# Linear attention and GELU layers on one core: state products of the fourth pair moved into its attention run, v of the first pair released by the first alpha

## The chip, the core and the metric

The kernel runs on one core of a Trainium2 chip. Five engines with queues of their own work side by side: TensorE (PE, with its weight loads PEld), VectorE (DVE), ScalarE (ACT), GpSimd (POOL) and SyncE (SP). The metric is the device time of one execution in microseconds (us); the time shown for a kernel is the median of its runs.

## What is computed

A gated linear attention recurrence over 768 tokens for 4 batches of 8 heads of 48 columns, then two dense layers (384 to 2048 to 384) with a tanh GELU between them, on all 3072 tokens:

```python
for t in range(S):
    state = alpha[:, :, t, :, None] * state + np.einsum('bhd,bhe->bhde', k[:, :, t], v[:, :, t])
    y[:, :, t] = np.einsum('bhd,bhde->bhe', q[:, :, t], state)
x = y.transpose(0, 2, 1, 3).reshape(B * S, H * D)
h = x @ w_in
g = 0.5 * h * (1.0 + np.tanh(c * (h + 0.044715 * h * h * h)))   # c = sqrt(2 / pi)
out = g @ w_out
```

## The kernel before, in words

Tokens are cut into six chunks of 128; a *pair* is two batches of one chunk, a *unit* one batch of it. There are twelve pairs, numbered from 0 (the first pair is pair 0, the fourth is pair 3); pair 2c + i holds batches 2i and 2i + 1 of chunk c.

One unit goes so. ACT takes the logarithm of alpha (`la`, L396 and L398); PE sums it over the tokens with a triangular matrix (`cum`, L383 and L387 for the packed pairs 0 and 1, L415 and L417 later); ACT makes b = exp(cum) and binv = exp(-cum) (L449) and, up to pair 2, the decay at the chunk's end (`bend`, L438). DVE makes q' = q b and k' = k binv (`qp`, `kp`, L477). Both are turned to have the columns on partitions: on PE with an identity and copied out of PSUM to `qkT` up to pair 4 (L487 and L518, copies L505 and L525), and from pair 5 on by a DMA transpose that SP issues (L545). In pairs 0 and 1 k' is also turned back to natural order (`kn`, L533, L540). The attention products k' q' (L582, `at`) are masked on DVE (L589, `atm`). The output y is the masked attention times v (L640, or L648 for a pair at once), and from chunk 1 on also q' times the carried state. The state is carried by a product of k' and v (L599, `kv`) and one or two DVE steps (L622, L625).

q' times the carried state is made in one of two ways. For pairs in the tuple `CARRIED` it stands inside the attention run: sixteen products of 64 rows by 48 columns (L562) into two PSUM banks that stay held until y is copied out as two parts of x (L658). For pair 3, not in the tuple, it is four products of 96 columns per unit (L637) in that unit's own y run (copy L664). x is turned (L671 and `xT` L675; by DMA L551 from pair 6 on) and feeds layer 1 (L683, `hT`), GELU on ACT (L689, `gT`), layer 2 (L702, `acc`), a copy (L714, `ot`) and the store (L727).

PSUM has three rings: `ff` (four banks: hT, acc, products of zeros, some sums and attention), `yk` (two banks: turns, state products, y) and `ca` (one pair of banks). `fill` (L317) multiplies zeros on PE into a spare bank; these results are not used.

The order of the work is decided when the program is built. A scheduler walks a hand-written list, `FIRST`, whose entries name an engine and a task (`P:cum0.0` is the sums of pair 0, unit 0, on PE; `P:fill.7` seven products of zeros), and places everything after it by the planner's costs (`W`, `COST`), due times (`prio`, changed by `SHIFT`) and extra dependences (`AFTER`). Each engine then runs its queue in that order, and waits only for semaphores. `LANDED` holds the times at which the planner takes the first 34 loads to have landed; it moves nothing on the chip but the plan.

Loads: a, q and k of the first two pairs are twelve strips, `load.0` to `load.11`, one batch each, issued by SP (one by ACT) at once in the order of `RINGS`; the last is k of pair 1, unit 1. All others stand in `LOADS`, on GpSimd's queue. A gate there is a one-column copy on GpSimd that waits for a tile, and so holds all that is queued behind it:

```python
def wait(self, r, m, j):
    u = self.p[list(self.p)[m]]
    return lambda e: self.nc.gpsimd.tensor_copy(self.gate[:, 0:1], u[r][:, j, 0, 0:1])
```

The first gate, `gatea 0 1`, waits for alpha of pair 0, unit 1, and lets v of pair 0 go (`load.12`, 384 KB). The second, `gatek 0 1`, waits for k of pair 0, unit 1, and lets the first quarter of `w_in` go, v of pair 1, the other weights and the later pairs.

Of the kernel before, what the change touches and what calls it, by code (L numbers as in the profile page):

```python
# [13 lines left out]

W = dict(**{'in': 2400},
    ln=745, exp=705, bend=170, gelu4=485, gelu2=340, table=1290,
    cum=530, cum_packed=1500, t8=450, t4=225, attn=340, kv=170, inter=165, intra=203, tx=168, l1_4=655, l1_2=340, l2=651,
    qk2=880, qk1=500, ev8=610, ev4=350, mask=610, st=1065, st0=545, end=110, attn2=600, vb=320, vb_act=480, ring=1300, ring_issue=670, out=2050, lead=600, receipt=1400, receipt_hw=1000, xc=475, xe=275, ot=540,
    ev8_act=920, ev4_act=520, xc_act=385, xe_act=400, ot_act=450,
    strip=1700, cast=1450, weight=2080, dma=2100, issue=1100, wissue=760, sp=420, store=2600, turn=1250, landed=2200, xbar_qk=1500, xbar_x=1400, turn_lead=50, stored=300, turn_receipt=200, rows=1826, ones=205, late_qk=1700, late_x=1700, late_x6=500, piece=330, late_k=1500, piece_issue=450, begin=620, cast_0=1300, share=1200, cast_1=1900, ln_packed=1040, cold=380, t64=640, fill=216, zero=1100,  # L20
)
COST = {
    ("ACT", "b"): (385, 135), ("ACT", "binv"): (385, 135), ("ACT", "ev"): (600, 40), ("ACT", "gelu"): (510, 110),
# [151 lines left out]
class _Kernel:  # L175
# [3 lines left out]

    SPLIT = (2,)  # L180
    EARLY = (0, 1)
    LOADS = ('gatea 0 1', 'v0', 'gatek 0 1', 'in 0', 'v1', 'in 1', 'in 2', 'in 3', 'out 0', 'out 1', '2a', 'out 2', '2b', 'out 3', '3', '4', '5', '6', 'a7', 'q7', 'hold k 5', 'k7', 'v7', 'a8', 'hold k 6', 'q8', 'k8', 'a9', 'hold k 7', 'v8', 'q9', 'k9', 'hold k 8', 'v9', 'a10', 'q10', 'hold x 7', 'k10', 'a11', 'hold k 9', 'q11', 'k11', 'v10', 'hold k 10', 'v11')

    PACKED, CUM_FF, R = (0, 1), (0, 1), 4
    RINGS = (('a', 0, 0, 1), ('a', 0, 1, 2), ('q', 0, 0, 1), ('k', 0, 0, 1), ('q', 0, 1, 2), ('k', 0, 1, 2),
# [1 line left out]
    BY_ACT = (2,)  # L187

    FIRST = """
        S:load.0 S:load.1 S:load.3 A:table.0 A:load.2 A:ln0.0 S:load.4 S:load.5 P:fill.7 G:gate.0 G:load.12 S:load.6 S:load.7 S:load.8 P:fill.2 P:cum0.0  # L190
        A:ln0.1 A:b0.0 P:cum0.1 V:qp0.0 P:t0.0 P:fill.1 A:binv0.0 A:bend0.0 V:kp0.0 S:load.9 A:b0.1 S:load.10 A:binv0.1 A:bend0.1 V:end0.0 V:qp0.1 V:kp0.1
        A:ev0.0 P:fill.3 P:t0.1 A:ev0.1 G:gate.1 P:t0.2 S:load.11 P:t0.3 A:ln1.0 V:ev0.2 G:load.13 G:load.14 A:ev0.3 P:attn0.0 A:ln1.1 V:mask0.0 V:mask0.1
        P:t0.4 P:t0.5 A:ev0.4 P:attn0.1 V:mask0.2 P:cum1.0 V:mask0.3 V:vb0.0 P:cum1.1 A:ev0.5 P:fill.1 P:fill.1 P:y0.0 G:load.15 P:kv0.0 G:load.16 A:binv1.0
        A:bend1.0 G:load.17 A:b1.0 V:vb0.1 A:x0.0 P:tx0.0 A:binv1.1 V:qp1.0 V:st0.0 A:bend1.1 A:b1.1 G:load.18 V:xe0.0 V:kp1.0 V:qp1.1 G:load.19 G:load.20
        P:fill.1 G:load.21 P:y0.1 P:t1.0 P:fill.1 V:end1.0 A:x0.1 P:t1.1 A:ev1.0 A:ev1.1 P:t1.2 G:load.22 V:kp1.1 P:tx0.1 V:xe0.1 P:attn1.0 A:ev1.2 G:load.23
        V:mask1.1 V:mask1.0 P:t1.3 P:kv0.1 A:ev1.3 V:st0.1 P:l10.0 P:t1.4 A:vb1.0 P:l10.1 A:vb1.1 V:ev1.4 P:y1.0 V:x1.0 P:attn1.1 P:t1.5 P:kv1.0 A:gelu0.0
        P:l10.3 V:mask1.3 V:mask1.2 A:ev1.5 P:l10.2 P:y1.1 A:gelu0.1 G:load.24 V:st1.0 A:gelu0.3 P:tx1.0 P:l10.5 A:gelu0.2 V:x1.1 A:gelu0.5 G:load.25 P:tx1.1
        V:xe1.0 V:xe1.1 P:l10.4 A:gelu0.4 P:l11.0 P:l11.3 G:load.26 G:load.27 A:gelu1.0 P:l10.6 P:l11.4 A:gelu1.3 G:load.28 P:l10.7 A:gelu0.6 A:gelu1.4
        A:gelu0.7 P:l11.1 P:l11.5 A:gelu1.1 P:l11.6 P:l11.2 A:gelu1.5 A:gelu1.6 A:gelu1.2 P:l11.7 A:gelu1.7 G:load.29 G:load.30 P:kv1.1 P:l20.2 A:ln2.0
        P:l20.6 P:l20.0 P:l20.3 P:cum2.0 A:binv2.0 A:b2.0 P:l20.1 G:load.31 P:l20.10 A:ln2.1 V:kp2.0 P:l20.4 V:qp2.0 P:t2.0 A:bend2.0 P:cum2.1 A:b2.1 P:l20.8  # L200
        P:l20.5 A:binv2.1 V:st1.1 P:l20.7 V:kp2.1 A:bend2.1 A:ev2.0 V:qp2.1 P:attn2.0 P:t2.1 A:ev2.1 G:load.32 V:mask2.1 P:l20.14 P:l20.12 A:ln3.0 V:mask2.0
        P:attn2.1 P:y2.0 P:l20.11 V:mask2.3 V:mask2.2 G:load.33 P:l20.9 A:ot0.0 A:x2.0 A:ot0.2 P:cum3.0 P:y2.1 A:b3.0 P:tx2.0 V:x2.1 P:l20.13 S:store0.0
        V:xe2.0 A:binv3.0 V:end2.0 P:tx2.1 P:l20.15 A:ot0.1 V:xe2.1 P:kv2.0 P:l12.0 A:ot0.3 V:qp3.0 V:st2.0 P:l12.3 P:l12.2 A:gelu2.0 A:gelu2.3 P:l12.1
        A:gelu2.2 S:store0.1 A:gelu2.1 V:kp3.0 S:store0.2 P:t3.0 P:l12.5 S:store0.3 A:ev3.0 P:l12.4 A:gelu2.4
    """.split()
    LANDED = {"load.0": 2830, "load.1": 3870, "load.2": 3320, "load.3": 5820, "load.4": 6330, "load.5": 6870, "load.6": 7670, "load.7": 8470, "load.8":
              9670, "load.9": 10370, "load.10": 11370, "load.11": 12070, "load.12": 10770, "load.13": 14170, "load.14": 16070, "load.15": 18070,
              "load.16": 19970, "load.17": 21870, "load.18": 23770, "load.19": 26170, "load.20": 26970, "load.21": 27670, "load.22": 28220, "load.23":
              28720, "load.24": 30620, "load.25": 31520, "load.26": 32220, "load.27": 32770, "load.28": 33270, "load.29": 35220, "load.30": 37020,
              "load.31": 38870, "load.32": 41230, "load.33": 42620}  # L210

    NARROW = (0, 1)

# [7 lines left out]

    XE_ACT = (3, 4, 5, 6, 7)

    CARRIED = (4, 5, 6, 7, 8, 9, 10, 11)

    AHEAD = ()

# [6 lines left out]
    PIECES = (0, 192, 320, 384)  # L234

    SHIFT = {
        'b10.0': 507, 'b8.0': 191, 'binv4.0': -2716, 'kp5.0': -87, 'kp9.0': -20, 'kv5.0': -409, 'kv9.0': 80, 'mask7.0': -200, 'mask8.0': 274,
        'mask8.1': 734, 'mask9.0': -233, 'qp6.0': 540, 'qp7.0': 50, 'rows4.0': 340, 'x4.0': 100,
    }

    AFTER = {
        'kv6.0': 'l25.4', 'kv7.0': 'l27.0', 'x3.0': 'binv4.0', 'y3.0': 'l22.3',
    }

    ROW_ENDS = (3, 4, 5, 6, 7, 8, 9)
# [484 lines left out]
    def tasks(self):  # L730
        s = self.s = Scheduler(self.BUFS, self.fill, 40000, self.FIRST, self.LANDED)
        B, NCH = self.B, self.NCH
# [28 lines left out]
        for r, m, lo, hi in self.RINGS:  # L761
            loads[r, m, lo] = loads[r, m, hi - 1] = s.add(
                "load", {"ACT" if n in self.BY_ACT else "SP": W["ring_issue"]}, n, self.load(r, *pairs[m], lo, hi), land=(W["ring_v" if r == "v" else "ring"] * (hi - lo) // 2 if n else W["begin"]))
            n += 1
        for step in self.LOADS:
            if step[0] in "aqkv" and step[1].isdigit():
# [20 lines left out]
        for m, (c, i) in enumerate(pairs):  # L787
# [66 lines left out]
            for j in range(2):  # L854
# [17 lines left out]
                if m in self.SINGLE or j:  # L872
                    units = (j,) if m in self.SINGLE else (0, 1)
                    apart = self.AT_FF.get(m, (0,))
                    carried = (c, 2 * i) if m in self.CARRIED else None
                    at = s.add("attn", {"PE": W["attn" if len(units) == 1 else "attn2"] + (230 if carried else 0)}, o + 1, self.attn(u, units, apart, carried),
# [8 lines left out]
            for j in range(2):  # L885
                b, o, k, ms, turned = 2 * i + j, P + 10 + 3 * j, kp[j], masks[j], turns[j]
                at = ats[m][-1 if m not in self.SINGLE else j]
                if m in self.CARRIED:
                    if j == 0:
# [3 lines left out]
                else:  # L893
                    y = s.add("y", {"PE": W["intra"] + (W["inter"] if c and m not in self.CARRIED else 0)}, P + 20 + j, self.y(u, j, c, b),
                              ms + turned + [vin[j]] + ([states[b, c - 1]] if c else []))
# [7 lines left out]
                else:  # L903
                    tx = s.add("tx", {"PE": W["tx"]}, P + 22 + j, self.turn_x(u, j), xcs)
                    xe = s.add("xe", {"DVE": W["xe"], **({"ACT": W["xe_act"]} if m in self.XE_ACT else {})}, P + 22 + j, self.turned_x(u, j, c, b), [tx])
                    tx.take("yk", xe)
                if m in self.CARRIED:
                    txs = (txs if j else []) + [tx]
# [165 lines left out]
```

## Time and profile before

| | us |
|---|---|
| runs | 172.65, 177.97, 176.06 (median 176.06) |
| the profiled execution, its own time | 172.84 |
| its span, first to last instruction | 171.1 |
| PE busy in it | 165.5 |
| ACT busy | 131.6 |
| DVE busy | 100.0 |

PE works through nearly the whole span, and its granted clock is full in all forty slices. Layer 1 (576 products) is 67.6 us of PE's time, layer 2 (416 products) 68.2 us. The DMA engines are busy at nine tenths or more until about half of the span.

How to read the profile: the page gives busy time by engine, tenths of busy time in forty slices, and groups of instructions by line. The chain of waits is followed back from the last instruction; a row of it has the start, the length, and the engine with the line. The timeline has the start, the length, engine, line, operation and tiles, and in brackets how long the engine was idle before and what ended that. The view by tile gives the time from issue to landing of a DMA, counted from the start of the issue.

### The profile page before, as it was taken

What the parts mean: (1) busy time and instruction counts of PE and PEld (TensorE: products, weight loads), DVE (VectorE), ACT (ScalarE), POOL (GpSimd) and SP (SyncE); (2) the same over time, 40 slices, a digit from 0 to 9 for tenths busy, and PEclk for the clock granted to TensorE, in tenths of its full rate; (3) what the DMA queues carried; (4) which work ended last, traced back from release to release, by engine and by line L of the source; (5) the groups of instructions that cost most, each with busy time, mean ns of one, the idle gap of its engine ahead of it and who ended that gap; (6) DMA issues with size and microseconds to landing.
All of it is one profiled execution on the core that took longest, in us unless ns stands there. A gap on an engine that the chain in (4) does not pass through costs nothing.

```text
span 171.1 us, 4471 instructions
## 1 busy us (share of the span) xinstructions
PE 165.5 (97%) x1852; PEld 130.3 (76%) x1853; DVE 100.0 (58%) x203; ACT 131.6 (77%) x221; POOL 58.9 (34%) x71
## 2 busy tenths in 40 slices
PE   7988999999999999999999999999999999999993
PEld 2665999666896887797797697797796796886973
DVE  6487920155987999895995797795840825100000
ACT  4687999848989897889969798399798992572831
POOL 2593546996647300807006106700703000000000
PEclk9999999999999999999999999999999999999999
DMA  4999999999999999999975999999699961401102
GB/s 132 271 274 243 209 245 231 227 239 195 233 304 227 242 241 145 173 160 196 222 149 116 224 174 117 236 250 181 163 141 178 145 158 28 138 0 50 46 0 92
DMA packets 53652, 29.91 MB, mean 175 GB/s; under 512 B 41728, under 2 KB 50048, under 8 KB 53632
## 3 DMA queue, kind: packets, MB, share of 16 engines
q0 software_dynamic: 26464, 17.70, 63.8%
q1 hardware_dynamic: 26896, 11.74, 35.8%
q8 instruction: 14, 0.23, 0.6%
q10 hardware_dynamic: 272, 0.20, 0.4%
q14 instruction: 6, 0.05, 0.1%
HBM read 25.17 MB, written 4.72 MB: 175 GB/s over the span
## 4 chain that ended last, share of the span: by engine, by line
PE 95%; ACT 2%; DVE 1%; issue 0%
PE hT L683 37%; PE acc L702 37%; PE at L582 4%; PE idle L317 3%; PE kv L599 2%; PE cum L415 2%; PE yps L648 2%; PE yps L562 1%; PE qkT_ps L487 1%; PE cum L383 1%; PE xT_ps L671 1%; ACT qkT L505 1%; PE yps L640 1%; PE k_ps L533 1%; PE qkT_ps L518 1%; ACT x L664 1%
## 5 line engine op out<-in xcount | busy, mean ns | idle before, releaser
L702 PE MATMUL acc<-w_out,gT 128*128 128x384 bf16 (+3 forms) x416 | 68.2, 314 | 0.0
L683 PE MATMUL hT<-xT,w_in 128*128 128x256 bf16 x576 | 67.6, 273 | 0.0
L683 PEld LDWEIGHTS <-w_in 128*128 128x128 bf16 x576 | 61.3, 114 | 1.4
L689 ACT ACTIVATE gT<-hT 128x512 bf16<-128x512 f32 x96 | 54.1, 603 | 7.4 <-PE hT L683 4.4
L702 PEld LDWEIGHTS <-gT 128*128 128x128 bf16 x416 | 37.5, 98 | 20.2
L589 DVE TENSOR_TENSOR atm<-at,ut 128x512 bf16<-128x512 f32 x48 | 30.0, 683 | 5.0 <-PE at L582 4.9
L714 ACT COPY ot<-acc 128x384 f32<-128x384 f32 (+3 forms) x24 | 10.8, 451 | 14.7 <-PE acc L702 13.2
L477 DVE TENSOR_TENSOR kp<-k,binv 128x768 bf16<-128x768 f32 (+1 forms) x15 | 11.8, 793 | 13.2 <-ACT binv L449 13.2
L350 POOL CAST gate<-qkT 128x1 f32<-128x1 bf16 x6 | 1.1, 190 | 50.6 <-DMA qkT<-kp 50.6
L477 DVE TENSOR_TENSOR qp<-q,b 128x768 bf16<-128x768 f32 (+1 forms) x15 | 11.9, 792 | 7.9 <-ACT b L449 7.9
L449 ACT ACTIVATE b<-cum 128x768 f32<-128x768 f32 (+1 forms) x15 | 10.3, 686 | 5.9 <-PE cum L415 3.9
L336 POOL DMA_DIRECT2D q<-in_q_dram x11 | 12.2, 1111 | 6.5 <-DMA w_in<-in_moe_w_in_dram 2.6
L336 POOL DMA_DIRECT2D vb<-in_v_dram x11 | 12.2, 1107 | 3.8 <-PE hT L683 1.5
L336 POOL DMA_DIRECT2D a<-in_alpha_dram x11 | 12.2, 1113 | 3.4 <-DMA w_in<-in_moe_w_in_dram 1.4
L336 POOL DMA_DIRECT2D k<-in_k_dram x11 | 12.2, 1108 | 3.3 <-DMA vb<-in_v_dram 2.1
L622 DVE TENSOR_TENSOR stmp<-kv,st 128x384 f32<-128x384 f32 x16 | 8.9, 554 | 6.4 <-PE kv L599 6.3
L465 DVE STREAM_TRANSPOSE rows<-b 32x256 f32<-32x256 f32 x28 | 12.3, 438 | 0.5
L308 ACT ACT_TABLE_LOAD x9 | 11.5, 1283 | 0.9 <-PEq L1058 0.7
L449 ACT ACTIVATE binv<-cum 128x768 bf16<-128x768 f32 (+1 forms) x15 | 10.3, 683 | 2.0 <-PE cum L415 1.1
L689 ACT ACT_TABLE_LOAD x9 | 11.5, 1283 | 0.2
L625 DVE TENSOR_TENSOR st<-stmp,ends 128x384 bf16<-128x384 f32 x16 | 9.0, 560 | 0.6
L398 ACT ACTIVATE la<-a 128x768 f16<-128x768 f32 (+1 forms) x11 | 8.6, 785 | 0.1
(83 smaller groups left out, 140.6 us busy)
## 6 DMA issues: line engine op xcount, KB each, us to landing
out_dram<-ot SPq DMA_DIRECT2D x19, 192.0 KB, 5.3
a<-in_alpha_dram POOLq DMA_DIRECT2D x9, 384.0 KB, 9.1
q<-in_q_dram POOLq DMA_DIRECT2D x9, 384.0 KB, 8.5
k<-in_k_dram POOLq DMA_DIRECT2D x9, 384.0 KB, 7.7
vb<-in_v_dram POOLq DMA_DIRECT2D x9, 192.0 KB, 9.6
w_in<-in_moe_w_in_dram POOLq DMA_DIRECT2D x4, 384.0 KB, 10.0
w_out<-in_moe_w_out_dram POOLq DMA_DIRECT2D x4, 384.0 KB, 11.4
out_dram<-ot SPq DMA_DIRECT2D x9, 96.0 KB, 5.8
```

Source lines behind the costliest of these rows:

```text
L308: nc.scalar.add_instruction(mybir.InstLoadActFuncSet(name=nc.get_next_instruction_name(), act_func_set_id=i, engine=mybir.EngineType.Activ ...
L336: dma(u[t][:, lo:hi].rearrange("t b h d -> t (b h) d"), src.rearrange("b h s d -> s (b h) d")[c * C:(c + 1) * C])
L449: self.nc.scalar.activation(u[n].rearrange("t i h d -> t i (h d)")[:, lo:hi], cum, AF.Exp, scale=1.0 if n == "b" else -1.0)
L465: nc.vector.transpose(t[f:f + 32], bass.AP(last.tensor, last.offset + o * D + 32 * half, [list(last.ap[0]), [2 * D, H], [1, 32]]))
L477: self.nc.vector.tensor_tensor(out, rows, b, op=ALU.mult)
L589: self.nc.vector.tensor_tensor(u["atm", i][:, o], u["at", i][o], self.ut[:, None, :].to_broadcast([self.C, self.H // 2, self.C]), op=ALU.mult)
L622: nc.vector.tensor_tensor(s, acc, old, op=ALU.add)
L625: nc.vector.tensor_tensor(new.rearrange("f p (o d) -> f (p o) d", o=2), acc.rearrange("f p (o d) -> f (p o) d", o=2), ends, op=ALU.mult)
L683: self.nc.tensor.matmul(h[:, s], w_in[:, j, nt % 4 + s], self.xT[c % self.NX][:, lo:hi, j], start=j == 0, stop=j == self.NKT - 1, skip_gro ...
L689: return lambda e: self.nc.scalar.activation(self.gT[c % self.NG][:, nt:nt + 2, lo * self.C:hi * self.C], f.pop(("h", c, lo, nt)), AF.Gelu ...
L702: self.nc.tensor.matmul(f["acc", c, b][:, lo:hi], self.gT[c % self.NG][:, nt, b * self.C:(b + 1) * self.C], self.w_out[:, nt, lo:hi], star ...
L714: self.copy(e)(f["ot", c, b][:, sl], f["acc", c, b] if half is None else f["acc", c, b, half][:, sl])
```

## The change

Four things, and the order that follows from them:

1. Pair 3 joins `CARRIED`, so its products of q' with the state go into its attention run as sixteen products, and its two y runs become one.
2. The first gate on GpSimd's queue waits for alpha of pair 0, unit 0, instead of unit 1.
3. `FIRST` is written anew. Seven products of zeros stand ahead of the first sums where nine stood; the two others come behind the first turn. The number of products of zeros is sixteen in both. Work is handed over between ACT and DVE: five copies (one vb, the x copies of pair 1, one x of pair 3, one xT of pair 4) go to ACT, eight (three qkT, three x, one xT, one result) to DVE.
4. The planner's costs for a packed sum (`cum_packed`, 1500 to 1700) and a product of zeros (`fill`, 216 to 250), `LANDED`, `SHIFT` and `AFTER` are new, and with them the places of some later tasks. The largest moves: the state product of pair 2, unit 1, from ahead of pair 3's attention to behind the second layer-1 task of chunk 1's second half; q' of pair 5 from ahead of pair 4's masks on DVE to behind them, and its DMA transpose with it; one state product each of pairs 7 and 8 by some layer-2 tasks; on GpSimd's queue v of pair 7 from behind alpha and q of pair 8 to ahead of them.

```diff
-    LOADS = ('gatea 0 1', 'v0', 'gatek 0 1', 'in 0', 'v1', 'in 1',
+    LOADS = ('gatea 0 0', 'v0', 'gatek 0 1', 'in 0', 'v1', 'in 1',
...
     FIRST = """
-        S:load.0 S:load.1 S:load.3 A:table.0 A:load.2 A:ln0.0 S:load.4 S:load.5 P:fill.7 G:gate.0 G:load.12 S:load.6 S:load.7 S:load.8 P:fill.2 P:cum0.0
-        A:ln0.1 A:b0.0 P:cum0.1 V:qp0.0 P:t0.0 P:fill.1 A:binv0.0 A:bend0.0 V:kp0.0 S:load.9 A:b0.1 S:load.10 A:binv0.1 A:bend0.1 V:end0.0 V:qp0.1 V:kp0.1
-        A:ev0.0 P:fill.3 P:t0.1 A:ev0.1 G:gate.1 P:t0.2 S:load.11 P:t0.3 A:ln1.0 V:ev0.2 G:load.13 G:load.14 A:ev0.3 P:attn0.0 A:ln1.1 V:mask0.0 V:mask0.1
+        A:table.0 A:load.2 S:load.0 S:load.1 S:load.3 S:load.4 A:ln0.0 S:load.5 P:fill.7 G:gate.0 G:load.12 A:ln0.1 P:cum0.0 A:b0.0 A:binv0.0 V:qp0.0 V:kp0.0
+        S:load.6 P:cum0.1 A:b0.1 A:binv0.1 S:load.7 A:bend0.0 P:t0.0 S:load.8 A:bend0.1 V:ev0.0 P:fill.2 P:t0.1 P:fill.1 V:qp0.1 S:load.9 S:load.10 V:kp0.1
+        P:fill.3 P:t0.2 G:gate.1 A:ev0.1 V:ev0.2 P:t0.3 P:attn0.0 V:mask0.0 V:end0.0 A:ln1.0 V:mask0.1 V:vb0.0 A:ev0.3 P:t0.4 A:ln1.1 A:ev0.4 P:attn0.1 P:t0.5
...
-    CARRIED = (4, 5, 6, 7, 8, 9, 10, 11)
+    CARRIED = (3,4,5,6,7,8,9,10,11)
     SHIFT = {
-        'b10.0': 507, 'b8.0': 191, 'binv4.0': -2716, 'kp5.0': -87, 'kp9.0': -20, 'kv5.0': -409, 'kv9.0': 80, 'mask7.0': -200, 'mask8.0': 274,
-        'mask8.1': 734, 'mask9.0': -233, 'qp6.0': 540, 'qp7.0': 50, 'rows4.0': 340, 'x4.0': 100,
+        'binv10.0': -10, 'binv8.0': -10, 'kp5.0': -164, 'kp7.0': -50, 'kp9.0': -30, 'kv5.1': -1267, 'mask3.0': 297, 'mask8.2': -662, 'mask8.3': -119,
+        'rows4.0': 731, 'rows5.0': -10, 'rows7.0': -603, 'tx3.1': 1088,
     }
     AFTER = {
-        'kv6.0': 'l25.4', 'kv7.0': 'l27.0', 'x3.0': 'binv4.0', 'y3.0': 'l22.3',
+        'kv2.1': 'l13.0', 'kv3.1': 'l22.6', 'kv6.0': 'l25.4', 'kv8.1': 'l28.3',
     }
```

## The prediction

> **What bounds the kernel now.** I read the page first: TensorE (PE) is busy for 97% of the span and the granted clock is full in every slice.
>
> ```profile
> span 171.1 us, 4471 instructions
> PE 165.5 (97%) x1852; PEld 130.3 (76%) x1853; DVE 100.0 (58%) x203; ACT 131.6 (77%) x221; POOL 58.9 (34%) x71
> PE   7988999999999999999999999999999999999993
> ```
>
> So all time without PE work is 171.1 - 165.5 = 5.6 us: 1.2 us before the first product, 2.8 us behind the last (168.26 to 171.1), and 1.6 us in the first slices, where the row of tenths falls below 9. The chain of waits in order of time says the same and gives the price of each block:
>
> ```profile
> 1.20 3.76 PE idle L317 x9
> 4.96 0.66 PE cum L383 x7
> ...
> 17.37 0.66 PE hT L683 x6
> ...
> 49.72 0.55 PE at L582 x16
> ...
> 53.65 0.17 PE yps L637 x4
> 53.82 0.20 PE yps L640 x8
> ...
> 63.63 0.30 PE yps L562 x16
> 63.94 0.45 PE at L582 x16
> ...
> 67.76 0.40 PE yps L648 x16
> ```
>
> From 17.37 us to 168.26 us this chain holds PE pieces only, without a wait. A change can therefore do three things: reach the first hT product earlier, take products out of PE, or open a hole behind 17.37 us. What paces the start is read in the timeline of the first 17 us, and for landings in the view by tile (the k strip of the first chunk's second pair, second unit, issued last of the twelve):
>
> ```profile
> 3.75 0.52 ACT L396 ACTIVATE la<-a 128x384 f16<-128x384 f32 x1 [1.73 <-DMA a<-in_alpha_dram]
> 5.06 0.52 ACT L396 ACTIVATE la<-a 128x384 f16<-128x384 f32 x1 [0.79 <-DMA a<-in_alpha_dram]
> 7.48 0.61 SPq L333 DMA_DIRECT2D k<-in_k_dram  x1
> 15.50 0.55 DVE L477 TENSOR_TENSOR kp<-k,binv 128x384 bf16<-128x384 f32 x1
> ```
>
> ```profile
> DMA to landing us min/median/max: 7.4/7.4/7.4
> ```
>
> The first alpha is through its logarithm at 3.75 + 0.52 = 4.27 us, but PE, behind nine products of zeros, takes the sums only at about 4.8. The last k strip lands at 7.48 + 7.4 = 14.9 us.
>
> **The start.** Seven zeros of 3.76 / 9 = 0.42 us each end near 4.1 us, so the sums of unit 0 start with the logarithm, at 4.3: 0.5 us earlier. Those of unit 1 wait for alpha of unit 1 (5.06 + 0.52 = 5.58) and stay. The exponentials and q' of unit 0 (0.49 and 0.56 us) move by 0.5; their turn then stands behind the sums of unit 1, 5.64 + 0.76 = 6.40 instead of 6.87. In its place two of the zeros run, and k' of unit 0 is turned behind them, no longer behind four (1.0 us). Units 0 and 1 thus run 0.3 to 0.5 us ahead. They cannot keep more than the last k strip allows. DVE now takes k' of pair 1, unit 1, before q' of that unit, so k' starts at landing, 14.9, and ends at 15.5. Behind it on PE stand its turn (0.23 us), one unit's attention (0.33), a zero (0.22), another turn (0.23) and a state product (0.17): 1.18, and the first hT product starts at about 16.75. It starts at 17.20 in the timeline of before (the chain counts it from the end of the state product, 17.37). Gain 0.45. Weights allow that: w_in's first quarter was issued at 7.88 and took 8.5 us, 16.4. I take 0.45; bounds 0 (the two rivals on clock and alpha) and 0.7, if the k strip lands 0.25 sooner because v fills the 0.77 DMA share of the stretch from 7 to 8 us. Zeros are sixteen in both.
>
> **v earlier.** GpSimd's gate waits for alpha of unit 0 (3.7 us) and no longer for unit 1 (5.0); behind it on POOL's queue stands v (issued at 5.21, landed 6.6 us later at 11.8), behind v the gate on k, which opened at 7.4 and still has to. So v moves by up to 1.3 us, the weights do not. The state and y products of unit 0, which waited for v's cast at 12.2, can go by 11 to 11.5. v's 384 KB are 1.2 us of wire at the 320 GB/s of those stretches, and that is taken from strips in flight: the rival on alpha.
>
> The Trainium skill, "Trainium Kernel Development and Optimization", Key Constraints, says that DMAs from the SP, ACT and POOL queues run on the same 16 engines and interleave, so that another issuer adds no bandwidth. Here the DMA share of the stretches from 5 to 12 us is 0.77 to 1.12, which agrees.
>
> **State products of pair 3.** Before: attention 0.55, two state products of four at 0.17, two y runs at 0.20, 1.29 us. After, as pair 4 does it: 0.30 + 0.45 + 0.40 = 1.15. Gain 0.14, all on PE. Both PSUM banks of the small tiles are now held from the attention to the two copies of x, so one pair-2 state product moves from 49.4 us to the next layer-1 run (near 58). Its state update (0.55 + 0.56 us on DVE) moves along; the state is wanted by pair 4 at 63.6. Cover: DVE loses one x copy (0.47) to ACT there and puts q' of pair 5 (0.87) behind pair 4's masks, so its load before those masks falls by 0.3. Without that cover pair 4's turns and attention would be 1.1 us late.
>
> **The rest of the new order** hands thirteen copies from ACT to DVE or back and reorders layer-2 runs; no PE work is added. ACT is full from 19 to 30 us (table, 16 gelu, one copy) and gets two x copies (0.38 from start to start, 13.29 to 13.67) for one k copy (0.46, 20.45 to 20.91): 0.3 more. Its eleven gelu from 23.28 on go at PE's pace, 0.65 for 0.60 of work, so 0.5 us of slack takes that. For holes of under 0.1 us I take +0.1 in all; bounds 0 and +0.3.
>
> **Sum.** -0.45 - 0.14 + 0.1 = -0.5 us. Against the profiled execution (172.84 us, 1.7 around its span): 172.3, span 170.6.
>
> **Rivals.** (1) *q' of pair 5 lands late*, the slower side. Its transpose is issued by SP once q' is made. Before, q' stood ahead of pair 4's masks:
>
> ```profile
> 60.70 0.95 DVE L477 TENSOR_TENSOR qp<-q,b 128x768 bf16<-128x768 f32 x1
> 62.94 3.02 SPq L545 DMA_TRANSPOSE qkT<-qp  x1
> ```
>
> Now it stands behind them. The masks ended at 64.70 + 2.48 = 67.2; less the gain, q' is done near 67.5. Pair 5's attention, 75.70 before, is due at 75.2. The transpose has 7.7 us. From issue to landing the four of that region took 5.3 to 9.1 us:
>
> ```profile
> DMA to landing us min/median/max: 5.3/7.0/9.1
> ```
>
> The 7.6 and 9.1 were two in flight together with loads queued on GpSimd; the later two, further apart, took 6.4 and 5.3. The late one now flies after its partner, so I take 6. Above 7.7 it decides: at 9.1 PE stands for 1.4 us, and the kernel is 0.9 slower than before (profiled 173.7).
>
> (2) *The slow clock lasts longer.* The first eight zeros start every 0.43 us, the four near 7.3 us took 0.86 together: PE begins at half speed and changes between 4.6 and 5.0. Seven zeros stop at 4.1 and leave PE idle for 0.2 us, and for up to 0.4 in front of the sums of unit 1. If the change comes only 3.4 us later, at 8, sums, turns and zeros before that take twice as long and the hT product comes back to 17.2: gain 0, total -0.04, 172.8. For it: the nine zeros just reach the change. Against it: the gap is short.
>
> The Trainium skill, "TensorE: Matmul & The Clock Gate", Part 1, states that the full clock comes after a busy window of about 3.4 us, and that the window is free-running. By that rule the change here, 3.4 to 3.8 us after the first product at 1.2, agrees, and seven zeros, 2.9 us, would fall short of it unless the sums count as well.
>
> (3) *v delays alpha of pair 1.* Its logarithm stands on ACT ahead of the copy that frees unit 1's attention. That alpha landed at 4.2 + 4.3 = 8.5; with 1.2 us of v ahead of it, 9.7, and the copy starts at 10.2, not 9.45. That eats the lead of unit 1 but meets the same k strip at 14.9; I price it at half the start's gain: -0.25, 172.6.
>
> **Numbers.** Forecast 0.55, late q' 0.20, clock 0.15, alpha 0.10. All lie within 1.5 us of before. What differs more are the runs: 172.65, 176.06 and 177.97, with the profiled one at 172.84, 3.2 below the median shown. The trace gives no cause for that. I therefore lay the -0.5 on the mean of the four executions, 174.9: 174.4 us. The range goes from the profiled execution less the full gain of 0.84 (172.0) to the slowest run with half of the forecast's gain (177.7), and holds the late q' on any run but that one. Two per cent, 3.5 us, is about what a measurement tells here from no change. No case of mine is worth that; a median among the low runs (172.3) would stand 2.1% under 176.06, and one among the high runs 2% over the low ones. Hence faster 0.22, within 0.63, slower 0.15.
>
> **What would show it.** Right: nine cold zeros become seven and the sums begin at 4.3; k' of pair 1, unit 1, starts at its landing near 14.9; the first hT product at 16.6 to 16.9; pair 3's attention with L562 ahead of L582 and no wait behind; PE without a hole to the end, its last product near 167.8. Wrong: half-speed sums at 5 us (clock); the second pair's logarithm idle until 9.5 (alpha); a wait of PE for a transposed qp near 75 us (late q'); or an hT product held by w_in's second quarter, which landed near 19.2.

## The result: slower by 0.45%, where 0.3% faster was forecast

| | before | after |
|---|---|---|
| median of 20 runs, us | 173.64 (172.5 to 177.97) | 173.95 (173.44 to 176.3) |
| ratio after to before, 95% interval | | 1.0045 [1.0025, 1.0066] |
| the profiled execution, its own time | 172.84 | 174.24 |
| its span | 171.1 | 172.5 |

The ratio is of the fast runs alone (17 and 19 of the 20, those not over 1.5% above their kernel's fastest), whose means lie 0.75 us apart, while the medians of all runs lie 0.31 us apart. The time lies in the forecast's range and within 2% of before, but it moved the other way. The profiled execution of before is 0.8 us faster than the median of its kernel, that of after 0.3 slower than its own, so the two traces differ by 1.4 us where the ratio is worth 0.45% of 173.6, 0.8 us.

The head of the page of after, the lines that were shown of before:

```profile
span 172.5 us, 4495 instructions
PE 166.2 (96%) x1861; PEld 130.4 (76%) x1861; DVE 101.7 (59%) x206; ACT 129.4 (75%) x218; POOL 59.2 (34%) x71
PE   7978999999999999999999999999999999999993
```

The span grew by 1.4 us, and only the first slices of PE differ. Next the chain of waits of after in order of time (start, length, what):

```profile
4.82 6.80 DMA a<-in_alpha_dram
...
11.65 0.52 ACT la L396
12.17 0.96 ACT kn L540 x2
...
15.60 0.37 PE yps L640 x8
...
51.61 0.30 PE yps L562 x16
51.91 0.45 PE at L582 x16
...
55.39 0.40 PE yps L648 x16
...
59.44 0.81 ACT b L449
...
60.97 1.28 ACT L689
...
62.91 2.12 PE hT L683 x18
```

Three things are to be seen. Pair 3 goes as pair 4 did before (L562, L582, and one L648 run of 0.40 for two of 0.20), as foreseen. Ahead of the first hT product the chain now runs through an alpha strip that took 6.80 us and through ACT; in before that strip wasn't in it. And behind 20 us the chain leaves PE once, at 59.4, for exponentials and a table load.

Where the difference arises is told by one product after the other. After less before, in us: first hT product 18.49 - 17.20 = +1.29; start of layer 2 of chunk 1's second half (52.29 - 50.89) +1.40; PE's last end (169.66 - 168.25) +1.41. So 1.3 of the 1.4 us is lost ahead of the first hT product.

The strip in the chain is alpha of pair 1, unit 1. The landings of its issue and the one before it, in the view by tile, first before, then after:

```profile
DMA to landing us min/median/max: 4.3/4.3/4.3
```

```profile
DMA to landing us min/median/max: 4.4/5.6/6.8
```

Unit 0's strip lands as before (8.5 us), unit 1's at 11.62 and not at 9.17. What moved instead is in the share of the DMA queues between 7 and 9 us (packets, MB, share of the 16 engines; the software queue is GpSimd's, which carries v, the hardware queue is SP's with the strips), before and after:

```profile
q1 hardware_dynamic: 600, 0.43, 70.9%
q0 software_dynamic: 25, 0.11, 21.0%
```

```profile
q0 software_dynamic: 84, 0.33, 69.3%
q1 hardware_dynamic: 256, 0.18, 29.1%
```

The stretch carries about as much in both (0.54 and 0.51 MB). v, issued at 3.98 and not at 5.21, takes 0.22 MB more of it, and the strips get 0.25 MB less. The Trainium skill, "DMA: Bandwidth & Descriptors", section "Issuing engines are not separate DMA queues", says that transfers from all issuers run on the same 16 engines and interleave; these shares agree. v's packets are the larger ones here: 84 for 0.33 MB are 3.9 KB each, where the strips' 256 for 0.18 MB are 0.7 KB each.

What the late strip holds is in the timeline of after (in brackets the idle time before, and what ended it):

```profile
11.65 0.52 ACT L396 ACTIVATE la<-a 128x384 f16<-128x384 f32 x1 [1.41 <-DMA a<-in_alpha_dram]
12.70 0.34 PE L599 MATMUL kv<-vb,kn 128*128 128x96 bf16 x4 [0.90 <-ACT kn L540]
```

ACT works in order. It stood 1.41 us idle at the logarithm of unit 1, and behind that in its queue stood the copies `kn` (L540), which need nothing of that alpha. The state product of pair 0 needs `kn`, and did not start before 12.70, though v had been cast at 11.8. Behind `kn` on ACT the exponentials, a copy of x and a vb follow back to back up to 15.6, where the second y run starts (14.22 before). Its copy `x` then stands on DVE ahead of k' of pair 1, unit 1, behind which the first hT product comes:

```profile
16.00 0.56 DVE L664 CAST x<-yps 128x384 bf16<-128x384 f32 x1 [0.47 <-PE yps L640]
16.60 0.56 DVE L477 TENSOR_TENSOR kp<-k,binv 128x384 bf16<-128x384 f32 x1
```

In this execution the last k strip was late as well: it landed at 16.50, 0.06 us before that copy ended, and would by itself have held the hT product nearly as long. This trace alone can't tell which of the two makes the kernel slower; the experiments have to.

### The profile page after: what moved, and what is told of

It reads as the page before. It is cut to its first block, busy times and chain, and to the rows that moved or that the text cites. A ratio compares the mean times of both kernels' runs of the same rounds, so it can differ in the third digit from the quotient of the medians.

```text
span 172.5 us, 4495 instructions
## 1 busy us (share of the span) xinstructions
PE 166.2 (96%) x1861; PEld 130.4 (76%) x1861; DVE 101.7 (59%) x206; ACT 129.4 (75%) x218; POOL 59.2 (34%) x71
## 4 chain that ended last, share of the span: by engine, by line
PE 85%; ACT 4%; DMA 4%; SPq 2%; DVE 2%; issue 0%
PE acc L702 37%; PE hT L683 35%; DMA a<-in_alpha_dram 4%; PE at L582 3%; SPq L333 2%; PE yps L648 2%; PE cum L415 2%; PE kv L599 2%; PE yps L562 2%; PE xT_ps L671 1%; ACT b L449 1%; DVE atm L589 1%; ACT L689 1%; PE yps L640 1%; ACT binv L449 1%; ACT kn L540 1%
## 5 line engine op out<-in xcount | busy, mean ns | idle before, releaser
L702 PE MATMUL acc<-w_out,gT 128*128 128x384 bf16 (+3 forms) x416 | 68.5, 314 | 0.0
L702 PEld LDWEIGHTS <-gT 128*128 128x128 bf16 x416 | 37.3, 98 | 20.1
L714 ACT COPY ot<-acc 128x384 f32<-128x384 f32 (+3 forms) x23 | 10.3, 451 | 15.0 <-PE acc L702 13.5
L477 DVE TENSOR_TENSOR qp<-q,b 128x768 bf16<-128x768 f32 (+1 forms) x15 | 11.9, 792 | 12.7 <-ACT b L449 12.6
L449 ACT ACTIVATE b<-cum 128x768 f32<-128x768 f32 (+1 forms) x15 | 10.3, 688 | 5.9 <-PE cum L415 3.2
L477 DVE TENSOR_TENSOR kp<-k,binv 128x768 bf16<-128x768 f32 (+1 forms) x15 | 11.9, 794 | 3.9 <-ACT binv L449 3.8
L308 ACT ACT_TABLE_LOAD x9 | 11.5, 1283 | 0.9 <-PEq L1058 0.7
L449 ACT ACTIVATE binv<-cum 128x768 bf16<-128x768 f32 (+1 forms) x15 | 10.3, 688 | 1.8 <-PE cum L417 0.9
L689 ACT ACT_TABLE_LOAD x9 | 11.5, 1283 | 0.2
```

What stands on the lines that cost most here:

```text
L308: nc.scalar.add_instruction(mybir.InstLoadActFuncSet(name=nc.get_next_instruction_name(), act_func_set_id=i, engine=mybir.EngineType.Activ ...
L449: self.nc.scalar.activation(u[n].rearrange("t i h d -> t i (h d)")[:, lo:hi], cum, AF.Exp, scale=1.0 if n == "b" else -1.0)
L477: self.nc.vector.tensor_tensor(out, rows, b, op=ALU.mult)
L689: return lambda e: self.nc.scalar.activation(self.gT[c % self.NG][:, nt:nt + 2, lo * self.C:hi * self.C], f.pop(("h", c, lo, nt)), AF.Gelu ...
L702: self.nc.tensor.matmul(f["acc", c, b][:, lo:hi], self.gT[c % self.NG][:, nt, b * self.C:(b + 1) * self.C], self.w_out[:, nt, lo:hi], star ...
L714: self.copy(e)(f["ot", c, b][:, sl], f["acc", c, b] if half is None else f["acc", c, b, half][:, sl])
```

## The experiments

The theory: releasing v 1.2 us earlier delays alpha of pair 1, and the time is lost because its logarithm holds ACT's queue ahead of the kn copies. The rivals: the seven zeros (sums on a slow clock), the last k strip, the release of the weights, and something in the order behind the start. The main readings, one profiled execution each (us), are set side by side. Names with a_ stand for kernels made from after, with b_ for those made from before; "gate" is what lets v go, "hT" the first hT product:

| kernel | gate | alpha of pair 1, unit 1 landed | kn starts | last k strip landed | first hT | median | ratio [95%] |
|---|---|---|---|---|---|---|---|
| before | unit 1 | 9.17 | 10.35 | 14.91 | 17.20 | 173.64 | 1 |
| after | unit 0 | 11.62 | 12.08 | 16.50 | 18.49 | 173.95 | 1.0045 [1.0025, 1.0066] |
| a_again | unit 0 | 11.39 | 11.84 | 15.42 | 18.12 | 173.98 | 1.0034 [1.0006, 1.0061] |
| a_gate_u1 | unit 1 | 9.31 | 10.58 | 16.20 | 18.19 | 173.72 | 1.0011 [0.9978, 1.0044] |
| b_gate_u0 | unit 0 | 11.75 | 12.21 | 15.79 | 18.67 | 174.20 | 1.0041 [1.0003, 1.0078] |
| b_gate_u0_ln_late | unit 0 | 11.11 | 10.97 | 13.26 | 18.00 | 173.87 | 1.0021 [1.0003, 1.0038] |
| b_gate_k0 | k of unit 0 | 8.92 | 10.32 | 14.36 | 17.55 | 173.68 | 0.9997 [0.9967, 1.0028] |
| b_seven | unit 1 | 8.98 | 10.46 | 14.39 | 17.31 | 173.37 | 0.9989 [0.996, 1.0018] |
| a_w_later | unit 0 | 11.85 | 12.30 | 13.90 | 18.58 | 173.93 | 1.0027 [1.0008, 1.0046] |
| b_start_a_rest | unit 1 | 9.10 | 10.72 | 17.06 | 18.13 | 173.69 | 0.9999 [0.9978, 1.002] |
| a_ln_late | unit 0 | 11.66 | 11.23 | 15.66 | 18.15 | 173.10 | 0.9983 [0.9963, 1.0002] |
| a_both_ln_late | unit 0 | 10.96 | 10.45 | 13.98 | 16.99 | 172.87 | 0.9984 [0.996, 1.0008] |
| a_both_again | unit 0 | 11.40 | 10.49 | 13.52 | 17.52 | 172.89 | 0.998 [0.9958, 1.0002] |
| a_gate_u1_ln_late | unit 1 | 9.19 | 9.93 | 13.76 | 17.27 | 173.62 | 1.0008 [0.9983, 1.0034] |
| a_three_mended | unit 0 | 10.98 | 10.65 | 13.15 | 17.12 | 173.40 | 1.0006 [0.9987, 1.0026] |
| b_start_a_rest_mended | unit 1 | 9.42 | 11.09 | 17.82 | 18.89 | 173.65 | 1.0027 [1.0004, 1.0051] |
| a_four_mended | unit 0 | 10.64 | 10.21 | 12.79 | 16.70 | 172.84 | 0.9988 [0.9962, 1.0013] |

Each ratio is to the runs of before on the same chip (medians 173.25 to 173.64). The last k strip does not go with the gate: it landed at 12.8 to 16.5 us in the ten traces with the gate on unit 0, and at 13.8 to 17.8 in the seven with a later one.

**The gate put back, in after.**

```diff
-    LOADS = ('gatea 0 0', 'v0', 'gatek 0 1', 'in 0', 'v1', 'in 1',
+    LOADS = ('gatea 0 1', 'v0', 'gatek 0 1', 'in 0', 'v1', 'in 1',
...
```

> The changed kernel with one thing undone: the first gate waits for alpha of unit 1 again, the order of all tasks as changed. Theory A (early v takes wire from the strips of pair 1): alpha of pair 1, unit 1, lands near 9.2 us instead of 11.6, the last k strip near 14.9 instead of 16.5, v near 11.9 instead of 11.2; ACT's wait of 1.4 us before the second logarithm of pair 1 is gone, and the first hT product comes about 0.9 us sooner (near 17.5, not 18.5): some 0.9 us faster than the changed kernel, within 0.3 us of before. Theory B (the new order itself is late): the hT product stays near 18.5 and the time at 1.004 of before.

Alpha landed at 9.31 again and kn started at 10.58, but in this execution the last k strip came only at 16.20; k' of that unit started at 16.29, and hT at 18.19. The median is 0.2 us below that of after; the interval of the ratio reaches from faster than before to that of after. The landing is settled by it, the time is not.

**The gate alone, in before.**

```diff
-    LOADS = ('gatea 0 1', 'v0', 'gatek 0 1', 'in 0', 'v1', 'in 1',
+    LOADS = ('gatea 0 0', 'v0', 'gatek 0 1', 'in 0', 'v1', 'in 1',
...
```

> The kernel before with only the first gate changed to alpha of unit 0; same order of tasks. Theory A: alpha of pair 1, unit 1, lands 2 to 2.5 us later than 9.2, the last k strip 1 to 1.6 us later than 14.9, the first hT product near 18.1 to 18.5 instead of 17.2; 0.9 to 1.3 us slower than before (1.005 to 1.007). Theory B: no change, ratio 0.998 to 1.002, since v, landing sooner, stands in nobody's way.

One entry of `LOADS` makes before slower by 0.4%, about what the whole change does. The order of events is that of after: alpha landed at 11.75, its logarithm ran at 11.78 after 1.01 us of idle time on ACT, and kn at 12.21. The rise of its profiled execution (175.6 us) is larger than that of its median, since PE also stood 1.22 us once at 109 us there, which no other trace has.

**Seven zeros ahead of the sums, in before; and v released later, in before.**

```diff
-... P:fill.2 P:cum0.0
+... P:cum0.0
...
-... P:t0.0 P:fill.1
+... P:t0.0 P:fill.2 P:fill.1
```

> The kernel before with seven products of zeros ahead of the first sums, the other two behind the first turn. Clock theory: the first sums start at 4.4 us at half speed, as in the changed kernel, and end no sooner than before; the first turn is 0.2 us late, and with six zeros behind it the second turn is 0.5 us late; the hT product 0.3 to 0.5 us late, ratio 1.002 to 1.003. Rival (the sums gain what the zeros free, as the prediction had it): the first turn 0.3 to 0.4 us sooner, ratio 0.998 to 1.000.

```diff
-    LOADS = ('gatea 0 1', 'v0', 'gatek 0 1', 'in 0', 'v1', 'in 1',
+    LOADS = ('gatek 0 0', 'v0', 'gatek 0 1', 'in 0', 'v1', 'in 1',
...
```

> The kernel before with the first gate moved the other way, to k of pair 0, unit 0, which landed at 6.2 us: v goes 1.2 us later. Theory A: the strips of pair 1 land sooner by up to 1 us (last k strip near 14, alpha of unit 1 at 9 or below), v lands near 13, and its cast becomes the wait of unit 0's y: hT between 17.0 and 17.9, ratio 1.000 to 1.004. If early transfers from GpSimd's queue do not slow the strips, these land as before and only v's delay shows: 0.5 us slower or more, strips unmoved.

Neither differs from before. By its interval, the seven zeros cost at most 0.2% and bring at most 0.4%. With the later gate v landed at 12.81, 0.95 us later than in before, and the ratio stayed 0.9997, at most 1.0028: no more than half of that delay can have reached the time, so v's landing was not, or not alone, what paced before's start.

**After once more, and with the weights let go later.** The second gate waits for alpha of pair 1, unit 0, and no longer for k.

> The changed kernel once more, as it is. Theory A: the landings are the change's and not this one execution's: alpha of pair 1, unit 1, again after 11 us, the last k strip again at 16 us or later, the first hT product between 18.1 and 18.7, ratio 1.003 to 1.006. Rival (scatter of landings from run to run): k strip anywhere from 14.4 to 16.5, as the five traces so far have it, and the hT product with it.

```diff
-    LOADS = ('gatea 0 0', 'v0', 'gatek 0 1', 'in 0', 'v1', 'in 1',
+    LOADS = ('gatea 0 0', 'v0', 'gatea 1 0', 'in 0', 'v1', 'in 1',
...
```

> The changed kernel with the second gate, the one ahead of the weights, on alpha of pair 1, unit 0 (landed at 8.5 us) instead of k of pair 0, unit 1 (7.6): w_in and v of pair 1 go 0.9 us later. If the strips' tail is slowed by the weights' packets: the last k strip lands 0.5 to 1 us sooner (15.5 to 16.0), the first hT product 0.4 to 0.9 us sooner, w_in's first quarter near 16.5. If it is not: k stays at 16.2 to 16.5, w_in is late, and the time does not fall.

The second trace of after has the same late alpha (11.39) and the same kn (11.84), with the k strip more than 1 us earlier than in the first. With the weights held back, the k strip landed at 13.90, earlier than in before, and hT still came at 18.58. In both traces k' waited for the `x` copy (16.24 and 16.70), not for its strip, and the ratio stayed at 1.003. So after is slower without a late k strip, and with the weights held back.

**The logarithm of unit 1 behind the kn copies, in after.**

```diff
-... A:ev0.3 P:t0.4 A:ln1.1 A:ev0.4 P:attn0.1 P:t0.5
+... A:ev0.3 P:t0.4 A:ev0.4 P:attn0.1 P:t0.5
...
-        P:cum1.0 P:kv0.0 V:mask0.2 S:load.11 A:ev0.5 P:y0.0
+        P:cum1.0 P:kv0.0 V:mask0.2 S:load.11 A:ev0.5 A:ln1.1 P:y0.0
```

> The changed kernel with the logarithm of pair 1, unit 1, moved on ACT's queue behind the two copies of kn that it stood ahead of. If the late alpha costs by holding up ACT's queue: the copies run at 10.4 us, the state product and y of unit 0 go near 11.8 instead of 12.7 and 13.2, and the first hT product comes 0.5 to 0.9 us sooner. If the last k strip (16.5 us) binds: y of unit 0 is sooner all the same, but the hT product stays within 0.2 us of k's landing plus 1.9, that is 18.2 to 18.5, and the time at 1.003 to 1.005.

The median fell by 0.88 us beside a_again of the same chip, and the intervals of the two ratios do not overlap, although alpha landed as late as ever (11.66). Its profiled execution (173.9) was the slowest of its twelve: there unit 0's alpha came late too, at 10.31, and its logarithm held the third turn's copy and with it kn (11.23), so that hT came at 18.15, no sooner than in a_again. That suggested the next kernel.

**Both logarithms behind the copies of their units; and unit 1's alone, with the old gate.** The first is a_ln_late with one move more:

```diff
-... V:end0.0 A:ln1.0 V:mask0.1 V:vb0.0 A:ev0.3 P:t0.4
+... V:end0.0 V:mask0.1 V:vb0.0 A:ev0.3 A:ln1.0 P:t0.4
```

> The changed kernel with both logarithms of pair 1 moved on ACT's queue: unit 0's behind the copy that frees unit 1's attention, unit 1's behind the two kn copies. Theory (v's packets delay alpha of pair 1, by 2.5 us for unit 1 in every execution and by 0 to 1.8 us for unit 0 in some, and ACT's queue hands that on): unit 1's attention no longer waits for unit 0's alpha, the hT product between 17.6 and 18.1, ratio 0.996 to 0.999, at least as good as with one logarithm moved. Rival (the gain of the one move was scatter): ratio 1.002 to 1.005.

> The changed kernel with the logarithm of pair 1, unit 1, behind the kn copies and the first gate back on unit 1. If the early release of v is worth something once ACT is not held up: slower than the same with the early gate (0.998), at 0.999 to 1.002, v's cast at 12.1 instead of 11.3. If early v is worth nothing and only the place of the logarithm counts: 0.998 again.

a_both_ln_late is 172.87, and again:

> The same kernel as a_both_ln_late (after, both logarithms of pair 1 behind the copies of their units), again and with more rounds. Then it was 0.9984 [0.996, 1.0008] of before. If the carried pair's 0.14 us and the earlier v together are worth something beside before: 0.997 to 0.999, with an interval below 1. If the first run was luck: 1.000 to 1.002. First hT product at 16.9 to 17.4, PE 151.15 us from there to its end.

172.89. Both medians lie below the fastest single run of after in its two series (173.44 and 173.3). Its timeline has the late strip without a wait before it:

```profile
10.49 1.08 ACT L540 COPY kn<-k_ps 128x512 bf16<-128x512 bf16 x2
11.47 0.53 ACT L396 ACTIVATE la<-a 128x384 f16<-128x384 f32 x1
17.52 0.82 PE L683 MATMUL hT<-xT,w_in 128*128 128x256 bf16 x6
```

Alpha landed at 11.40 here, 0.2 us before that of after, but the copies ran ahead of it. Against before, the two ratios are 0.9984 and 0.998, each with an interval that just holds 1; taken as independent, their mean is 0.9982 with a half-width of sqrt(0.0024^2 + 0.0022^2) / 2 = 0.0016. That it beats after is shown (the interval of a_both_again lies below both of after); that it beats before, by some 0.3 us, is likely and no more.

a_gate_u1_ln_late moves unit 1's logarithm alone and so stands beside a_ln_late. With the logarithms where after has them, the early gate gave 1.0045 and 1.0034, the old one 1.0011; with that of unit 1 behind the copies, the early gate gave 0.9983 and the old one 1.0008. The move is worth 0.5 to 0.6% where alpha comes late, and nothing that can be told where it comes in time. So what it takes away is the wait for the late strip. The early v seems to be worth 0.25% once it holds nobody (0.9983 beside 1.0008), but these two intervals overlap.

**Both logarithms moved in before's order, with the early gate.**

```diff
-... P:t0.3 A:ln1.0 V:ev0.2 G:load.13 G:load.14 A:ev0.3 P:attn0.0 A:ln1.1
+... P:t0.3 V:ev0.2 G:load.13 G:load.14 A:ev0.3 A:ln1.0 P:attn0.0
...
-... P:cum1.1 A:ev0.5 P:fill.1
+... A:ev0.5 A:ln1.1 P:cum1.1 P:fill.1
```

> Before, with the first gate on alpha of unit 0, and both logarithms of pair 1 moved on ACT behind the copies that stood behind them (that of unit 0 behind the third turn's copy, that of unit 1 behind the second kn copy). The gate alone gave 1.0041 of before, with alpha of unit 1 landing at 11.75 us instead of 9.2 and its logarithm holding the kn copies. Theory 'the late alpha costs only by holding ACT': alpha of unit 1 is late again (11.0 to 11.9 us), the kn copies no longer wait for it, the first hT product comes at 17.2 to 17.6 and not at 18.67, ratio 0.997 to 1.001, below that of the gate alone. Rival 'the gate costs by the strips themselves or by the sums of unit 1, wherever the logarithm stands': hT at 18.2 or later, ratio 1.003 to 1.005.

Between both expectations: 1.0021 and hT at 18.00. kn came 1.24 us earlier than with the gate alone and hT 0.67. In both profiled executions, though, the first exponential started at 6.35 and 6.46 us, not at 5.73 as in before, because the sums ran on the slow clock (last section), so some 0.6 us of what is left has another cause in the trace; whether also in the medians isn't known. The rest is in the chain of waits:

```profile
12.04 0.43 ACT la L396
...
12.51 0.82 PE cum L383 x7
...
13.86 0.21 PE yps L640 x8
```

In before's order the sums of pair 1, unit 1, stand on PE ahead of the first y run. Alpha landed at 11.11, the logarithm, now behind the copies, ended at 12.47, the sums started at 12.51 (11.52 in before) and the y run came behind them. So here the late logarithm holds PE's queue. In after's order that y run stands ahead of the sums. In before's order the cast of v stands on DVE behind all four masks of pair 0 and started at 12.80, so the early v can bring nothing there. That holding ACT is the larger part of the gate's cost is shown in after's order. In before's it is not: the two intervals overlap, and the medians stand 0.57 us (gate alone) and 0.62 us (logarithms moved) above those of before on their chips.

**The rest of the new order behind before's start.** Before's first tasks, gate and zeros, then after's order, pair 3 carried.

```diff
-    CARRIED = (4, 5, 6, 7, 8, 9, 10, 11)
+    CARRIED = (3,4,5,6,7,8,9,10,11)
...
+        ... P:attn3.0 A:gelu2.7 P:l22.0 V:mask3.1 P:l22.1 V:mask3.2
...
```

> The order of before up to where its hand-written list ends (gate on unit 1, nine zeros), and behind it the changed kernel's order with pair 3's state products inside its attention run. If all of the loss lies in the start: hT near 17.2 to 17.5, PE's products from there to the end 0.14 us shorter, one hole of 0.15 us at layer 1's fifth task of chunk 1's second half, so within 0.1 us of before in the trace and a ratio of 0.998 to 1.002. If the rest costs too: 1.003 or more, with a hole of over 0.3 us behind 45 us.

0.9999: the part behind the start neither gains nor loses what this many runs can tell. Its hT product came at 18.13, later than foreseen, behind a k strip that landed at 17.06. In the trace PE took 151.04 us from the first hT product to its last end, before 151.05.

**The small hole near 62.5 us.** In after PE stands 0.145 us at the fifth hT run of chunk 1's second half. Two kernels put the sums of pair 5 ahead of the last layer-2 run before it: a_three_mended, on a_both_ln_late (there also, on DVE, a mask ahead of a state update), and b_start_a_rest_mended, on b_start_a_rest with seven zeros first:

```diff
-... P:tx3.1 A:ln5.0 P:l22.7 V:xe3.1 P:kv3.1 P:cum5.0
+... P:tx3.1 A:ln5.0 P:cum5.0 P:l22.7 V:xe3.1 P:kv3.1
```

> The changed kernel with both logarithms moved, the sums of pair 5 ahead of the last layer-2 task of pair 3's block instead of behind it, and the mask of pair 1 that frees the attention bank ahead of a state update. Theory: the holes of 0.13 us at pair 1's second attention and of 0.145 us at the fifth layer-1 task near 62 us go, so from the first hT product to PE's last it takes 150.9 us (151.04 before, 151.16 changed); with the hT product as in the run with both logarithms moved, ratio 0.994 to 0.998. Rival (PE is late there for another reason): 151.1 or more.

> The start of before (gate on unit 1) with seven zeros ahead of the first sums and two behind the first turn, and the changed kernel's rest with pair 5's sums ahead of the last layer-2 task. Theory: 150.9 us from the first hT product to PE's last, hT at 17.2 to 18.1 as k lands; 0.14 us faster than before by the trace, ratio 0.997 to 1.001. If seven zeros cost: hT 0.3 us later than in the other runs with that start, ratio over 1.001.

Both miss: 1.0006 [0.9987, 1.0026] and 1.0027 [1.0004, 1.0051]. The hole grew to 0.40 us in both, and PE took 151.72 and 151.40 us from its first hT product, where 150.9 was foreseen; the hole at pair 1's second attention, which the mask was to close, grew from 0.14 to 0.25. In the second, hT came at 18.89, set by a k strip that landed at 17.82, so it does not tell what seven zeros cost. The chain of a_three_mended shows what made the large hole:

```profile
56.99 1.26 issue
58.25 0.48 ACT ot L746
58.73 0.72 ACT b L481
```

On ACT the copy of the last layer-2 run (`ot`) stands ahead of the exponential. The moved sums pushed that run back by 0.33 us, and the exponential, whose input had been ready, waited behind the copy. So the copy was moved as well:

```diff
-... A:ot2.1 V:kp4.0 P:l13.0 A:b5.0 S:store2.1 V:st3.1 P:l13.1 A:binv5.0 P:kv2.1
+... V:kp4.0 P:l13.0 A:b5.0 V:st3.1 P:l13.1 A:binv5.0 A:ot2.1 S:store2.1 P:kv2.1
```

> a_both_ln_late, with the sums of pair 5 on PE ahead of the last layer-2 run of chunk 1's second half (as in a_three_mended) and, on ACT, the copy of that run's result moved behind both exponentials of pair 5. Theory: the hole at l13.4 (0.145 us in after, 0.40 in a_three_mended) was made by the exponential waiting behind that copy; with the copy behind it the hole is 0.05 us or less, PE takes 151.0 to 151.05 us from the first hT product to its end, ratio 0.1% below a_both_again. Rival: the hole is ACT's load there as such (gelu late by what stands before it in any order), hole 0.1 to 0.2 us, ratio that of a_both_again.

The hole is gone, as the theory had it: the chain of waits from 53 to 63 us now holds PE pieces only.

```profile
56.46 0.43 PE cum L447 x2
56.90 0.65 PE acc L734 x4
```

The time, 172.84 us and 0.9988 [0.9962, 1.0013], does not show it beside a_both_again: PE took 151.08 us from its first hT product, where a_both_again took 151.15, and that is under what twelve runs tell. (In these written-out orders the line numbers are 32 higher: L447 is L415, L734 is L702.)

## Why the prediction was wrong, by its steps

**The base.** The -0.5 us was laid on the mean of four executions (174.9), two of which, 176.06 and 177.97, stood far above the kernel's usual 173.6. The forecast of 174.4 is near the measured 173.95 by that luck alone; its gain of 0.3% did not come.

**The start, -0.45: the step that failed.** Measured, +1.29 at the first hT product. The step had k' of pair 1, unit 1, start when its strip lands, 14.9, and the hT product 1.85 us behind it. The 1.85 was right (1.88 to 1.91 in the ten traces with after's start). The start of k' was not: it came at 16.60 in after, and at 16.24 and 16.70 in a_again and a_w_later, 0.8 and 2.8 us after the strip had landed. What it waited for was the `x` copy on DVE, the end of the series that the late alpha had held up on ACT. That the last k strip is the wall that everything meets was not so even in before, whose chain of waits to the first hT product does not hold it, but ACT's copies:

```profile
14.62 0.48 ACT x L664
15.10 1.07 ACT qkT L505 x2
...
16.21 0.33 PE xT_ps L671 x3
```

With that wall in the sum, whatever delays alpha could be priced only as lost lead ahead of it. Rival (3) had the right mechanism: v takes the engines, alpha of pair 1 comes late, its logarithm holds ACT. It had the size and the place wrong. It let unit 0's strip bear 1.2 us of v (reckoned at 320 GB/s, the best of those stretches; their mean from 5 to 12 us, 284, gives 1.4); in the ten traces with the gate on unit 0, unit 1's landed at 10.6 to 11.9, in the seven with a later gate at 8.9 to 9.4, up to 2.9 us apart, and unit 0's at 8.5 to 10.3 against 8.1 to 8.5. And it stopped at the copy that frees unit 1's attention; behind the second logarithm stand the kn copies and, in after's order, ACT's whole series up to the second y run, which has no slack to the first hT product. And the landing of the last k strip is no fixed number: it was anywhere from 12.8 to 17.8 us in the seventeen traces, and decided in some (a_gate_u1, 16.20, with k' at 16.29).

**Zeros and clock.** "The sums of unit 0 start with the logarithm, at 4.3" came out at 4.40, but their seven products took 1.44 us where they had taken 0.82, and the first turn came at 7.10, not earlier than 6.87. That is rival (2) in this execution. Over the runs of b_seven, seven zeros cost at most 0.2% (0.9989 [0.996, 1.0018]), so they are not the main reason for the result.

**v earlier.** It landed 0.64 us earlier (11.22 for 11.86), not up to 1.3. Its cast moved from 12.18 to 11.28, and that part was right; "can go by 11 to 11.5" failed for the state product, which waited for kn until 12.70.

**Pair 3, -0.14, and the rest, +0.1.** The first is right as far as the traces tell: the pieces are 0.30, 0.45 and 0.40, and PE, from the first hT product to its end, takes 151.16 us in after with two holes of 0.137 and 0.145, hence 150.88 without them, where before takes 151.05: -0.17. The holes are a mis-sized term, 0.28 for 0.1, within its bound of 0.3. One is the exponential of pair 5 described above, the other a mask of pair 1 that comes late at 19.9. Together the part behind the start comes to +0.11, and 1.29 + 0.11 = 1.40 is the whole difference of the spans.

**Late q' (rival 1, on which the slower side rested).** It did not happen. The transpose of pair 5's q' was issued at 69.37, landed after 5.4 us at 74.75, and the attention took it at 77.03. The 6 us assumed was near. The slower side came true by another mechanism.

## What to carry to other kernels

Where an in-order engine has instructions that wait for a DMA, look at what is queued behind them that doesn't need that DMA: such a wait was free while the strip came in time, and cost 0.5% when a neighbour's transfer was released 1.2 us earlier. When a load is started earlier, price it by the strips issued while it is in flight and by the in-order queue behind each of their users, not by the bytes against the last landing. Where such a wait is moved back, look also at who waits for its result: in before's order that was PE's queue, and nothing was seen to be gained. And a landing time read from one trace is a draw, not a limit: take a second trace before a sum is built on it.

## What the runs showed of the hardware

How late a strip comes is partly systematic and partly chance. Alpha of unit 1 separates cleanly by the gate (above), while the last k strip, issued between 7.46 and 7.66 us in all, spread over 5 us between executions.

PE's change from the slow to the full rate at the start comes at different times in different executions. It can be read off the seven products of the first sums (L383) and the seven of the second, since their work is fixed: together they take 0.82 us at the full rate and 1.44 at the slow one. In the timeline of before, and of b_start_a_rest_mended:

```profile
5.64 0.82 PE L383 MATMUL cum<-la,ut_blk 128*128 128x384 f16 x7
```

```profile
4.42 1.44 PE L415 MATMUL cum<-la,ut_blk 128*128 128x384 f16 x7
5.80 1.44 PE L415 MATMUL cum<-la,ut_blk 128*128 128x384 f16 x7
```

The first products start at 1.19 us in all. The change came before 4.46 in b_seven (seven zeros, sums at 0.82 from there) and after 7.0 in b_start_a_rest_mended and a_gate_u1 (both sums at 1.44); with nine zeros it came at 4.6 in before and above 5.6 in b_gate_u0, whose first sums took 1.34. So the number of zeros does not set it. The Trainium skill, "TensorE: Matmul & The Clock Gate", Part 1, says that the window of about 3.4 us which decides is free-running and does not reset when the kernel starts; a change that comes from under 3.3 to over 5.8 us after the first product agrees with that. The variation of 500 ns to either side that the section gives does not: the spread here is over 2.5 us. The granted clock of the profile shows 1.00 through these slices, so the change does not show in it.
